# Weights of an attention and gated feed-forward kernel stored raw in the first batch and split in the second, with four small edits around the scores and the softmax

## The chip, the cores and the metric

The kernel runs on one NeuronCore of one Trainium2 chip. The metric is the device time of one launch in microseconds (us), taken as the median of three runs. TensorE is called PE here, its weight loads PEld, VectorE DVE, ScalarE ACT, GpSimd POOL; SP is the queue from which nearly all DMAs are issued.

## The reference

Causal attention over 4 batches, 12 heads, 448 positions and a head size of 64, then a gated feed-forward block of width 1536 on the 1792 rows of 768:

```python
scores = scale * np.matmul(q, k.transpose(0, 1, 3, 2))
scores = np.where(mask, -1000000000.0, scores)
scores = scores - np.max(scores, axis=-1, keepdims=True)
attn = np.exp(scores)
attn = attn / (np.sum(attn, axis=-1, keepdims=True) + 1e-09)
x = np.matmul(attn, v)   # regrouped to (4*448, 768)
g = x @ w_gate
out = (g * (1.0 / (1.0 + np.exp(-g))) * (x @ w_val)) @ w_out
```

All inputs and the output are float32.

## The kernel before, in words

**Precision.** Most products are made with two float32r parts: a number is copied to float32r (its high part), the copy is subtracted from the number (its low part), and a product takes three matmuls: high by high, high by low, low by high. In the code this is `mm3` (L871) for the feed-forward block and the list `passes` (L486) for the scores. Batch 0's attention alone works in plain float32 (`NS`, `NP`, L30).

**Stages.** The four batches are worked one after another. A batch has twelve attention units, one for each head, that come in pairs; the feed-forward block of a batch takes its 768 rows of attention output `xs`, split into `xh` and `xl` (L785), and runs 24 column groups `M` (L888) and six output groups `MO` (L924). Attention of batch c+1 is interleaved with the feed-forward block of batch c.

**One attention unit.** PE makes the scores S (L485). DVE adds the mask and takes the row maximum (L548), ACT takes the exponential and sums each row into a tile `sums` (L563), DVE adds 1e-9 and takes the reciprocal `rec` (`recip`, L573 to L577), ACT or POOL or DVE multiplies by it (L607 to L617), PE transposes the result into a PSUM tile T (L694), and the transposed probabilities are split into `ph` and `pl` (`spread`, L627). The next transposes use the same PSUM bank, so they wait until DVE has read T for `pl`. Then PE multiplies with the values (L734). `sums` and `rec` are rings of `NR` rows; unit u uses row u mod NR.

**Weights.** A feed-forward group needs one 128 by 768 block of weights in two parts, `whl` (five buffers). The weights arrive 64 bits wide in `wide` (three buffers); ACT or POOL takes the upper part (`upper`, L851), DVE joins it with the lower (`lower`, L854) into the float32 block `wraw` (two buffers), and `split` (L811) copies and subtracts. This is done for the 36 blocks in batch 0. `RAW` (L46) is the list of batches that split their weights and store both parts to a scratch in HBM (`keep`, L820): with `[0]`, batch 0 stores 768 KB for each block, and the batches 1 to 3 load 768 KB for each block and split nothing. A batch ahead of the one in `RAW` stores the float32 block alone (`wr`, 384 KB).

**What sets the order.** A planner (`Planner.run`, L104) places every operation on an engine by due times and a table of costs (`cost`, L64; `TURN`, L42, for changes between kinds of work on PE), picks the engine where several are allowed, and writes one order for all engines. Each engine and the SP queue run theirs strictly in that order; waits are on semaphores. So a change in the costs moves instructions everywhere.

**The start.** 22 small bfloat16 matmuls on a tile of ones (`WARM`, L279) run on PE while the first inputs load. Then come the scores of the first unit pair, then those of the second.

**Short blocks.** The queries are cut at 64, 192, 320 and 448. The first block has 64 rows only; its weight load is made `FEW` = 72 columns wide (L504), as is that of the low parts of the probabilities against the values (L740).

Of the kernel before, what the change touches and what calls it, by code (L numbers as in the profile page):

```python
# [8 lines left out]
F32 = mybir.dt.float32  # L9
# [8 lines left out]
P = 128  # L18
# [2 lines left out]
CUTS = [[0, 64, 192, 320, 448], [0, 64, 192, 320, 448], [0, 64, 192, 320, 448], [0, 64, 192, 320, 448]]  # L21
WID = [0, 64, 192, 320, 448]
CHUNKS = [[(0, 0, 448)], [(1, 0, 448)], [(2, 0, 448)], [(3, 0, 448)]]
NR = 8
SLOPE0 = 1.0
WLEAD = 1.2
XD = [-10.0, 3.0]
# [11 lines left out]
SHARED = 0.5  # L39
PVLATE = 0  # L40
LAT = {"PE": 0.29, "DVE": 0.2, "ACT": 0.23, "POOL": 0.2, "SP": 0.1}
TURN = {'ms': 0.19, 'sm': 0.19, 'mt': 0.0, 'tm': 0.0, 'ts': 0.19, 'st': 0.19, 'mv': 0.15, 'vm': 0.15, 'tv': 0.15, 'vt': 0.15, 'sv': 0.15, 'vs': 0.15, 'om': 0.055, 'os': 0.1, 'so': 0.19, 'ot': 0.03}  # L42
TS = 0.0
PF = 1.12
GF = 1.25
RAW = [0]  # L46
SG = [[[0, 3]], [[1, 2]]]
TV = 0.0
WINDOW = 96
SPARE = [2]  # L50
FEW = 72
WARM = 22
FIRST = [[[0, 1]], [[2]], [[3]]]
KBUS = 1 / 320
DLAT = 1.8
# [8 lines left out]
def cost(e, kind, n):  # L64
    if e == "ACT":
        return {"psum": 66, "sbuf": 110, "ptr": 190, "exp": 280, "tanh": 160}[kind] / 1e3 + n / 1200
    if e == "DVE":
        return 0.075 + n / {"one": 1920}.get(kind, 960)
    if e == "POOL":
        return {"one": 190, "ptr": 260, "two": 180}[kind] / 1e3 + n / {"two": 465.0}.get(kind, 1200.0)  # L70
    return {"r": max(n * 0.4475e-3 + 0.0025, 0.109), "n": n / 600, "t": n * 0.109 / 128}[kind] + 0.001


class Res:
# [154 lines left out]
def kernel(  # L229
# [33 lines left out]
    masks = cpool.tile([P, P + maskX + P], F32, tag="masks", name="masks")  # L263
    back, mask = masks[:, : maskX + P], masks[:, P:]
    both = cpool.tile([P, D], F32, tag="both", name="both")
    all_sums = cpool.tile([P, NR, NKC], F32, tag="sums", name="sums")
    sums = [all_sums[:, i] for i in range(NR)]
    all_rec = cpool.tile([P, NR, NKC], F32, tag="rec", name="rec")
    rec = [all_rec[:, i] for i in range(NR)]
    xs = [cpool.tile([P, T], F32, tag=f"xs{i}", name=f"xs{i}") for i in range(KD)]  # L270
    xh = [cpool.tile([P, T], F32R, tag=f"xh{i}", name=f"xh{i}") for i in range(KD)]
# [4 lines left out]
    ones = xs[0][:, : P // 2]  # L276
    nc.vector.memset(ones, 1.0)
    warm = bank("O", "warm")
    for _ in range(WARM):  # L279
        nc.tensor.matmul(warm[:, :P], ones.bitcast(BF16), ones.bitcast(BF16), start=True, stop=True)  # L280
    cpool.tile([P, 32], F32, tag="pad", name="pad")
    top = cpool.tile([P, WC], U32, tag="top", name="top")
    nc.vector.memset(top, 0)
    nc.vector.memset(all_sums, 1.0)
    make_identity(nc, ident)
    nc.gpsimd.memset(masks, 0.0)
    for m_, step, base in ((back, 1, 1 - P), (mask, -1, maskX)):
# [104 lines left out]
    def attention(u):  # L392
# [76 lines left out]
        if h % 2 == 0:  # L469
# [10 lines left out]
            for gi_, sess in enumerate(FIRST if rest else SG if c == 0 else [sum(SG, [])]):  # L480
# [4 lines left out]
                def score(gi_=gi_, sess=sess, steps=steps, tags=tags):  # L485
                    passes = ((None, None),) if U.ns else ((0, 0), (0, 1), (1, 0))  # L486
                    for x, blks in enumerate(sess):
                        for y in (0, 1):
                            B_, off = bank(tags[x], f"S{u + y}_{gi_}_{x}"), 0
                            for i in blks:  # L490
                                q1_ = U.qi[i][1][1]
                                st[u + y][f"S{i}"] = B_[:, off : off + q1_]
                                off += q1_
                    for i in steps:
                        q0, q1_ = U.qi[i][1]
                        for z, (a, b_) in enumerate(passes):
                            for y in (0, 1):
                                half = slice(D * y, D * y + D)
                                Q = s["qw"][half] if U.ns else s["Q"][half, a]
                                K = s["kw"][half] if U.ns else s["K"][half, b_]  # L500
                                if U.joint and i == 0:
                                    nc.tensor.matmul(st[u]["S0"][half], Q[:, :D], K[:, :D] if y else K[:, S - D :], start=True, stop=True)
                                    continue
                                r = max(U.rows[i], FEW)  # L504
                                nc.tensor.matmul(st[u + y][f"S{i}"][:r], Q[:, q0 : q0 + r],  # L505
                                                 K[:, :q1_] if y else K[:, S - q1_ :], start=z == 0, stop=z == len(passes) - 1)
                ws = [U.qi[i][1][1] for i in steps]
                if U.ns:
                    so = op({"PE": (sum(cost("PE", "n", w) + 0.06 for w in ws) + TS, score), "kind": "s"}, due(2),
                            (rest if gi_ else some) or [lq, lk], list(rSs.values()), [rq, rk])  # L510
                else:
                    so = op({"PE": (sum(3 * cost("PE", "r", w) for w in ws) + TS, score), "kind": "s"}, due(2), sp,
                            list(rSs.values()), [rQ, rK])
                for x, blks in enumerate(sess):
                    for i in blks:
# [56 lines left out]

        def recip():  # L573
            i0, i1 = U.own[0][0], U.own[-1][0] + 1
            sm, rc = sums[u % NR][:, i0:i1], rec[u % NR][:, i0:i1]
            nc.vector.tensor_scalar(rc, sm, 1.0e-9, None, ALU.add)
            nc.vector.reciprocal(rc, rc)  # L577
        rc = op({"DVE": (0.3, recip)}, due(5), exps, [], [rsum])

# [138 lines left out]
    def weigh(u):  # L718
# [6 lines left out]
        if not npv:  # L725
            rO, dps, use, dur = Res("O"), [], [], 0.0
            for g, o_, w, _, stk, d_, r_ in (blocks[j] for j in range(nj)):
                dps += [x for x in d_ if x not in dps]
                use += [r for r in r_ if r not in use]
                dur += (1 if stk else 2) * cost("PE", "r", w)  # L730

            todo = [(j, "ph") for j in (0, *range(2, nj))] + [(j, "pl") for j in range(nj - 1, 0, -1)] + [(1, "ph")]

# [282 lines left out]
```

## Time and profile before

| | |
|---|---|
| median of three runs | 683.66 us (683.42 to 683.88) |
| the profiled execution, its own time | 684.65 us |
| its span, first to last instruction | 682.9 us |
| PE matmul busy | 671.8 us, 98% of the span |
| PE weight loads busy | 598.9 us, 88% |
| DVE, ACT, POOL busy | 356.7 us, 347.8 us, 193.7 us |
| moved by DMA | 165.08 MB, 242 GB/s over the span |

The profile is one execution. Busy matmul time is modelled, since matmuls overlap. The idle time in front of an instruction is shown with what released it. The mean over the span hides the stages: batch 0's weights are prepared in the first third, and the last fifth has feed-forward work alone.

### The profile page before, as it was taken

How to read it: one execution, taken by the hardware profiler on the slowest of the kernel's cores; microseconds unless marked ns; L12 is line 12 of the kernel's file. 1: busy time of each engine (PE TensorE's matmuls, PEld its weight loads, DVE VectorE, ACT ScalarE, POOL GpSimd, SP SyncE). 2: the span in 40 equal slices, each digit the busy share in tenths (PEclk: the TensorE clock that was granted, in tenths of full speed). 3: DMA queues.
4: the chain of work that ended last, by engine and by line, in shares of the span. 5: the costliest groups of instructions: out<-in, count | busy, mean ns of one | idle time of the engine just before them, and what ended most of it. 6: DMA issues, size and time to landing. Idle time of an engine off the chain costs nothing.

```text
span 682.9 us, 10861 instructions
## 1 busy us (share of the span) xinstructions
PE 671.8 (98%) x3898; PEld 598.9 (88%) x3898; DVE 356.7 (52%) x881; ACT 347.8 (51%) x864; POOL 193.7 (28%) x238
## 2 busy tenths in 40 slices
PE   9999999999999999999999999999999999999998
PEld 6567898899888999999999989999999999999997
DVE  5777889898788464355633346545444222222100
ACT  6998688687798363245634336346345211111000
POOL 3766455556162130031322214134232000000000
PEclk9999999999999999999999999999999999999999
DMA  8878899999988865556667665554555675676771
GB/s 293 277 260 308 303 352 390 321 374 314 347 309 324 320 202 201 191 176 215 202 223 239 201 230 189 200 186 139 186 198 164 216 224 213 223 229 212 226 251 41
DMA packets 40118, 165.08 MB, mean 242 GB/s; under 512 B 4480, under 2 KB 13952, under 8 KB 40064
## 3 DMA queue, kind: packets, MB, share of 16 engines
q1 hardware_dynamic: 39904, 164.28, 70.6%
q8 instruction: 31, 0.51, 0.3%
q14 instruction: 23, 0.19, 0.1%
q10 hardware_dynamic: 160, 0.10, 0.1%
HBM read 130.55 MB, written 33.82 MB: 241 GB/s over the span
## 4 chain that ended last, share of the span: by engine, by line
PE 81%; ACT 11%; DVE 6%; issue 1%; POOL 0%; ACTq 0%; DVEq 0%
PE M L874 15%; PE M L875 15%; PE M L876 15%; PE MO L874 8%; PE MO L875 8%; PE MO L876 7%; PE S L505 4%; PE O L741 4%; ACT p L565 4%; PE T L699 3%; ACT p L609 2%; ACT ph L311 1%; ACT top L311 1%; DVE wraw L857 1%; PE T L667 1%
## 5 line engine op out<-in xcount | busy, mean ns | idle before, releaser
L874 PE MATMUL M<-xh,whl 128*128 128x448 f32 x576 | 215.0, 373 | 0.0
L875 PE MATMUL M<-xl,whl 128*128 128x448 f32 x576 | 209.4, 364 | 0.0
L876 PE MATMUL M<-xh,whl 128*128 128x448 f32 x576 | 209.1, 363 | 0.0
L874 PEld LDWEIGHTS M<-xh,whl 128*128 128x128 f32 x576 | 108.2, 188 | 8.5 <-issue 1.7
L876 PEld LDWEIGHTS M<-xh,whl 128*128 128x128 f32 x576 | 108.1, 188 | 7.7
L875 PEld LDWEIGHTS M<-xl,whl 128*128 128x128 f32 x576 | 108.4, 188 | 6.8 <-DVE xl L333 0.3
L874 PE MATMUL MO<-hh,whl 128*128 128x448 f32 x288 | 107.2, 372 | 0.0
L876 PE MATMUL MO<-hh,whl 128*128 128x448 f32 x288 | 104.6, 363 | 0.6 <-DVE whl L333 0.6
L875 PE MATMUL MO<-hl,whl 128*128 128x448 f32 x288 | 104.7, 364 | 0.0
L565 ACT ACTIVATE p<-p,m 128x192 f32<-128x192 f32 (+3 forms) x180 | 91.1, 509 | 3.4 <-DVE m L553 3.3
L311 ACT ACTIVATE ph<-T 128x384 fp32r<-128x384 f32 (+3 forms) x116 | 57.8, 504 | 56.5 <-PE T L667 34.4
L553 DVE CUSTOM_DVE_ANT_0 p<-S,masks 128x192 f32<-128x192 f32 (+3 forms) x180 | 68.3, 426 | 21.4 <-PE S L505 20.2
L311 ACT ACTIVATE hh<-t 128x448 fp32r<-128x448 f32 x40 | 23.1, 577 | 82.0 <-DVE t L917 82.0
L609 ACT ACTIVATE p<-p,rec 128x192 f32<-128x192 f32 (+3 forms) x130 | 58.8, 502 | 9.3 <-DVE rec L577 9.0
L911 DVE SCALAR_TENSOR_TENSOR t<-t,M 128x448 f32<-128x448 f32 x48 | 29.7, 619 | 57.2 <-ACT t L907 56.8
L876 PEld LDWEIGHTS MO<-hh,whl 128*128 128x128 f32 x288 | 54.0, 188 | 4.7 <-DVE whl L333 1.0
L874 PEld LDWEIGHTS MO<-hh,whl 128*128 128x128 f32 x288 | 54.1, 188 | 4.5 <-issue 1.2
L875 PEld LDWEIGHTS MO<-hl,whl 128*128 128x128 f32 x288 | 54.2, 188 | 3.6 <-DVE hl L333 0.3
L917 DVE TENSOR_TENSOR t<-t,M 128x448 f32<-128x448 f32 x48 | 29.6, 618 | 51.0 <-PE M L876 50.6
L907 ACT ACTIVATE t<-M 128x448 f32<-128x448 f32 x48 | 26.0, 542 | 57.5 <-PE M L876 56.9
L333 DVE TENSOR_TENSOR pl<-T,ph 128x384 fp32r<-128x384 f32 x72 | 39.6, 550 | 22.6 <-ACT ph L311 22.3
L699 PE MATMUL T<-ident,p 128*128 128x128 f32 x288 | 46.8, 276 | 3.3 <-DVE pl L333 3.0
(80 smaller groups left out, 822.7 us busy)
## 6 DMA issues: line engine op xcount, KB each, us to landing
whl<-ws SPq DMA_DIRECT2D x108, 768.0 KB, 4.4
wide<-in_w_dram SPq DMA_DIRECT2D x36, 768.0 KB, 6.8
ws<-whl SPq DMA_DIRECT2D x36, 768.0 KB, 7.5
vraw<-in_v_dram SPq DMA_DIRECT2D x24, 256.0 KB, 4.3
out_dram<-osb SPq DMA_DIRECT2D x24, 224.0 KB, 4.7
qraw<-in_q_dram SPq DMA_DIRECT2D x23, 224.0 KB, 4.6
kraw<-in_k_dram SPq DMA_DIRECT2D x23, 224.0 KB, 4.6
qraw<-in_q_dram SPq DMA_DIRECT2D x1, 128.0 KB, 2.5
```

The source lines that it names most:

```text
L311: nc.scalar.activation(out(), in_(), AF.Copy, scale=scale)
L333: r["DVE"] = (cost("DVE", "two", n), lambda: nc.vector.tensor_tensor(out(), a(), b(), alu))
L505: nc.tensor.matmul(st[u + y][f"S{i}"][:r], Q[:, q0 : q0 + r], K[:, :q1_] if y else K[:, S - q1_ :], start=z == 0, stop=z == len(passes) - 1)
L553: nc.vector.tensor_tensor_reduce(p[:r], s[f"S{i}"][:r], mask[:r, maskX - q0 : maskX - q0 + q1_] if h % 2 else back[:r, P - min(q1_, P) : P ...
L565: nc.scalar.activation(p[:r], p[:r], AF.Exp, bias=peak(i)[:r], scale=-1.0, accum_out=sums[u % NR][:r, i : i + 1],)
L609: nc.scalar.activation(p[:r], p[:r], AF.Copy, scale=rec[u % NR][:r, i : i + 1])
L699: nc.tensor.transpose(pt[:, o_ + q0 - bs : o_ + q0 - bs + r], s[f"p{i}"][:r, k0 : k0 + P], ident[:r, :r])
L874: nc.tensor.matmul(out[:, :n], a[:, w], xhi, start=first, stop=False)
L875: nc.tensor.matmul(out[:, :n], a[:, w], xlo, start=False, stop=False)
L876: nc.tensor.matmul(out[:, :n], l[:, w], xhi, start=False, stop=last)
L911: nc.vector.scalar_tensor_tensor(t, t, 1.0, ps[c, f, 0][:, :N], ALU.add, ALU.mult)
L917: nc.vector.tensor_tensor(t, t, ps[c, f, 1][:, :N], ALU.mult)
```

## The change

In batch 0 each weight block is now stored as one float32 block of 384 KB. Batch 1 loads that block, splits it again (36 copies and 36 subtractions of 128 by 768) and stores both parts; the batches 2 and 3 load both parts as before. Eight more small matmuls follow the first unit pair's scores. The addition of 1e-9 becomes a sum of pairs: a row `NR` of `sums` holds 1e-9, and a `tensor_reduce` adds that row to the unit's row; NR goes from 8 to 7. `FEW` goes from 72 to 66. The planner has other costs for changes between kinds of work on PE, for the 64-wide scores and for the products with the values.

```diff
-NR = 8
+NR = 7
-TURN = {'ms': 0.19, 'sm': 0.19, 'mt': 0.0, 'tm': 0.0, 'ts': 0.19, 'st': 0.19, ...
+TURN = {'ms': 0.15, 'sm': 0.17, 'mt': 0.0, 'tm': 0.0, 'ts': 0.15, 'st': 0.17, ...
-RAW = [0]
+RAW = [1]
-FEW = 72
+FEW = 66
+WARM2 = 8
...
-    return {"r": max(n * 0.4475e-3 + 0.0025, 0.109), "n": n / 600, "t": n * 0.109 / 128}[kind] + 0.001
+    return {"r": max(n * 0.4475e-3 + 0.0025, 0.109), "f": n * 0.4475e-3 + 0.0045, "n": n / 600, "t": n * 0.109 / 128}[kind] + 0.001
...
-    all_sums = cpool.tile([P, NR, NKC], F32, tag="sums", name="sums")
+    all_sums = cpool.tile([P, NR + 1, NKC], F32, tag="sums", name="sums")
...
+    busy(WARM)
...
-    nc.vector.memset(all_sums, 1.0)
+    nc.vector.memset(all_sums[:, :NR], 1.0)
+    nc.vector.memset(all_sums[:, NR], 1.0e-9)
...
+                    if u == 0 and i in FIRST[-1][0]:
+
+                        busy(WARM2)
...
-                    so = op({"PE": (sum(3 * cost("PE", "r", w) for w in ws) + TS, score), "kind": "s"}, due(2), sp,
+                    so = op({"PE": (sum(3 * (0.062 if w == D else cost("PE", "r", w)) for w in ws) + TS, score), "kind": "s"}, due(2), sp,
...
-            sm, rc = sums[u % NR][:, i0:i1], rec[u % NR][:, i0:i1]
-            nc.vector.tensor_scalar(rc, sm, 1.0e-9, None, ALU.add)
+
+            sm, rc = all_sums[:, u % NR :: NR - u % NR, i0:i1], rec[u % NR][:, i0:i1]
+            nc.vector.tensor_reduce(rc, sm.rearrange("p a c -> p c a"), mybir.AxisListType.X, ALU.add)
             nc.vector.reciprocal(rc, rc)
...
-                dur += (1 if stk else 2) * cost("PE", "r", w)
+                dur += (1 if stk else 2) * cost("PE", "f", w)
```

The order moves on every engine. Three places follow.

DVE at the end of batch 0's weights (before): `whl33` to `whl35` are the low parts of the last three blocks, `p24` the masked scores of the first unit of batch 2, `ph22_0` and `ph23_0` the low parts of the transposed probabilities of the last unit pair of batch 1.

```order
408 L553 ISA m25_2715 128x1
409 L333 TENSOR_TENSOR whl33_2694<-wraw33_2683,whl33_2694 128x768
410 L553 ISA p24_3_2675,m25_2715<-S25_0_0_2607,masks_67 128x448
411 L553 ISA m25_2715 128x1
412 L857 SCALAR_TENSOR_TENSOR wraw34_2756<-wide34_2592,top_138 128x768
413 L576 TENSOR_SCALAR rec_70<-sums_69 128x4
414 L577 RECIPROCAL rec_70<-rec_70 128x4
415 L333 TENSOR_TENSOR whl34_2765<-wraw34_2756,whl34_2765 128x768
416 L857 SCALAR_TENSOR_TENSOR wraw35_2817<-wide35_2640,top_138 128x768
417 L545 MEMSET p26_0_2824 64x128
418 L333 TENSOR_TENSOR ph22_0_2815<-T23_0_2780,ph22_0_2815 64x448
419 L333 TENSOR_TENSOR ph23_0_2820<-T23_0_2780,ph23_0_2820 64x448
```

The same place after the change:

```order
400 L339 TENSOR_TENSOR pl22_1_2653<-T22_1_2625,ph22_1_2644 128x384
401 L867 SCALAR_TENSOR_TENSOR wraw34_2661<-wide34_2475,top_138 128x768
402 L339 TENSOR_TENSOR whl33_2642<-wraw33_2620,whl33_2642 128x768
403 L339 TENSOR_TENSOR pl22_2_2691<-T22_2_2664,ph22_2_2684 128x384
404 L867 SCALAR_TENSOR_TENSOR wraw35_2700<-wide35_2580,top_138 128x768
405 L339 TENSOR_TENSOR whl34_2686<-wraw34_2661,whl34_2686 128x768
406 L339 TENSOR_TENSOR xl4_87<-xs4_75,xh4_81 128x448
407 L339 TENSOR_TENSOR whl35_2709<-wraw35_2700,whl35_2709 128x768
408 L554 MEMSET p26_0_2741 64x128
409 L339 TENSOR_TENSOR ph22_0_2743<-T23_0_2728,ph22_0_2743 64x448
410 L339 TENSOR_TENSOR ph23_0_2749<-T23_0_2728,ph23_0_2749 64x448
411 L339 TENSOR_TENSOR whl36_2755<-wraw36_2719,whl36_2755 128x768
```

The last blocks of batch 0 now come ahead of the scores of unit 24, and all of them, up to `whl35`, ahead of `ph22_0`; before, unit 24 and 25 stood in front of `whl33`.

DVE in batch 1 (before), where unit 27's T bank is read: `t1_4` is the gated product of feed-forward group 4, `xs1` the attention output.

```order
499 L333 TENSOR_TENSOR ph27_0_3379<-T27_0_3364,ph27_0_3379 64x448
500 L333 TENSOR_TENSOR hl4_105<-t1_4_3350,hh4_93 128x448
501 L333 TENSOR_TENSOR xs1_72<-O26_3392,tmp26_3407 64x448
502 L333 TENSOR_TENSOR pl27_1_3421<-T27_1_3403,ph27_1_3414 128x384
503 L333 TENSOR_TENSOR pl27_2_3445<-T27_2_3426,ph27_2_3435 128x384
```

The same place after the change:

```order
497 L339 TENSOR_TENSOR ph27_0_3365<-T27_0_3347,ph27_0_3365 64x448
498 L339 TENSOR_TENSOR whl48_3372<-wraw48_3307,whl48_3372 128x768
499 L320 TENSOR_SCALAR ph27_1_3398<-T27_1_3389 128x384
500 L339 TENSOR_TENSOR xs1_72<-O26_3378,tmp26_3393 64x448
501 L339 TENSOR_TENSOR pl27_1_3413<-T27_1_3389,ph27_1_3398 128x384
502 L339 TENSOR_TENSOR whl49_3419<-wraw49_3360,whl49_3419 128x768
503 L339 TENSOR_TENSOR pl27_2_3442<-T27_2_3421,ph27_2_3431 128x384
```

A subtraction of 128 by 768 now stands in front of `ph27_1` and another between `pl27_1` and `pl27_2`. In the whole of batch 1, DVE has 33 such subtractions and POOL 3; ACT has 23 of the copies and POOL 13.

PE near the end of batch 0's attention (before): T9 are the transposes of unit 9, O9 its product with the values, M0_1 a feed-forward group of batch 0.

```order
196 L699 MATMUL T9_2_782<-ident_66,p8_2_615 128x128
197 L699 MATMUL T9_2_782<-ident_66,p8_3_618 128x128 x2
198 L874 MATMUL M0_1_792<-xh0_77,whl1_607 128x448
199 L875 MATMUL M0_1_792<-xl0_83,whl1_607 128x448
200 L876 MATMUL M0_1_792<-xh0_77,whl1_607 128x448
201 L772 MATMUL O9_800<-ph9_0_786,vraw8_547 64x64 x2
```

The same place after the change:

```order
212 L709 MATMUL T9_2_783<-ident_66,p8_2_621 128x128
213 L709 MATMUL T9_2_783<-ident_66,p8_3_605 128x128 x2
214 L782 MATMUL O9_798<-ph9_0_788,vraw8_555 64x64 x2
215 L782 MATMUL O9_798<-ph9_0_788,vraw8_555 64x384 x2
```

The three feed-forward matmuls between the transposes and the product are gone from there; they come later.

## Rows read from the trace of the kernel before

**Rows 1.** The page, busy time and share of the span by engine.

```profile
PE 671.8 (98%) x3898; PEld 598.9 (88%) x3898; DVE 356.7 (52%) x881; ACT 347.8 (51%) x864; POOL 193.7 (28%) x238
```

**Rows 2.** Stretches: busy us of PE, PEld, DVE, ACT, POOL; clock, DMA share, GB/s.

```profile
193.00:226.00 33.00, 31.51 (x210) 27.61 (x210) 28.29 (x73) 30.38 (x83) 15.74 (x18) 1.00 0.89 316
226.00:280.00 54.00, 54.00 (x297) 50.03 (x296) 25.66 (x60) 20.33 (x47) 8.31 (x14) 1.00 0.65 221
```

**Rows 3.** Waits of PE: engine, line, releaser, us in total, times, longest.

```profile
PE T L699 <- DVE pl L333: 3.0, 4, 1.4
```

**Rows 4.** Lines 576 and 577: duration in ns, shortest, median, longest.

```profile
L576 DVE TENSOR_SCALAR rec<-sums x48: 151/170/1625, 9.3 to 527.8; 128x4 f32<-128x4 f32 x42, 128x3 f32<-128x3 f32 x6
...
L577 DVE RECIPROCAL rec<-rec x48: 175/178/179, 9.5 to 528.0; 128x4 f32<-128x4 f32 x42, 128x3 f32<-128x3 f32 x6
```

**Rows 5.** Timeline near 67 us: start, length, engine, line, then idle time before.

```profile
66.55 1.82 POOL L336 TENSOR_TENSOR whl<-wraw,whl 128x768 fp32r<-128x768 f32 x1
...
66.78 1.62 DVE L576 TENSOR_SCALAR rec<-sums 128x4 f32<-128x4 f32 x1 [0.18 <-ACT p L565]
...
69.20 0.30 PE L699 MATMUL T<-ident,p 128*128 128x128 f32 x1 [1.40 <-DVE pl L333]
```

**Rows 6.** Timeline near 396 us.

```profile
395.12 1.14 DVE L576 TENSOR_SCALAR rec<-sums 128x4 f32<-128x4 f32 x1
...
397.06 0.30 PE L699 MATMUL T<-ident,p 128*128 128x128 f32 x1 [0.64 <-DVE pl L333]
```

**Rows 7.** Timeline near 502 us.

```profile
501.24 0.77 DVE L576 TENSOR_SCALAR rec<-sums 128x4 f32<-128x4 f32 x1
...
502.81 0.41 PE L699 MATMUL T<-ident,p 128*128 128x128 f32 x2 [0.28 <-DVE pl L333]
```

**Rows 8.** Timeline near 210 to 218 us.

```profile
209.81 1.01 DVE L576 TENSOR_SCALAR rec<-sums 128x4 f32<-128x4 f32 x1 [0.19 <-ACT p L565]
...
215.17 1.72 DVE L333 TENSOR_TENSOR whl<-wraw,whl 128x768 fp32r<-128x768 f32 x1
...
218.36 0.55 PE L699 MATMUL T<-ident,p 128*128 128x128 f32 x3 [0.65 <-DVE pl L333]
```

**Rows 9.** Timeline near 203 us.

```profile
202.11 1.91 DVE L333 TENSOR_TENSOR whl<-wraw,whl 128x768 fp32r<-128x768 f32 x1
...
204.06 0.47 PE L876 MATMUL MO<-hh,whl 128*128 128x448 f32 x1 [0.62 <-DVE whl L333]
```

**Rows 10.** Timeline of PE at the start, and the same scores near 27 us.

```profile
0.98 2.53 PE L280 MATMUL warm<-xs 128*128 128x128 bf16 x22 [0.98 <-DVE xs L277]
...
8.54 0.48 PE L502 MATMUL S<-kraw,qraw 64*64 64x64 f32 x4 [0.61 <-DVE m L553]
8.95 3.57 PE L505 MATMUL S<-kraw,qraw 64*128 64x448 f32 x12
...
27.35 1.89 PE L505 MATMUL S<-kraw,qraw 64*128 64x448 f32 x12
```

**Rows 11.** Weight loads by shape: busy us, mean ns of one.

```profile
L505 PEld LDWEIGHTS S<-KS,QS 64*128 64x128 f32 x324 | 22.7, 186 | 0.3
...
L505 PEld LDWEIGHTS S<-KS,QS 64*72 64x72 f32 x108 | 4.8, 139 | 4.6 <-issue 4.6
```

**Rows 12.** The subtractions of the weights on DVE, all in batch 0.

```profile
L333 DVE TENSOR_TENSOR whl<-wraw,whl 128x768 fp32r<-128x768 f32 x28 | 31.6, 1129 | 0.9 <-ACT whl L311 0.9
...
L333 DVE TENSOR_TENSOR whl<-wraw,whl x28: 928/951/1916, 35.2 to 215.2; 128x768 fp32r<-128x768 f32 x28
```

**Rows 13.** DMA issues: count, KB each, median us to landing.

```profile
ws<-whl SPq DMA_DIRECT2D x36, 768.0 KB, 7.5
```

**Rows 14.** Timeline of PE near 45 us: two feed-forward matmuls, then O9.

```profile
45.05 0.37 PE L875 MATMUL M<-xl,whl 128*128 128x448 f32 x1
45.26 0.37 PE L876 MATMUL M<-xh,whl 128*128 128x448 f32 x1
45.91 1.78 PE L772 MATMUL O<-ph,vraw 64*64 64x64 f32 x12 [0.28 <-ACT ph L311]
```

More of the change, by code (lines that the diff above doesn't have):

```diff
@@ L41 @@
 LAT = {"PE": 0.29, "DVE": 0.2, "ACT": 0.23, "POOL": 0.2, "SP": 0.1}
-TURN = {'ms': 0.19, 'sm': 0.19, 'mt': 0.0, 'tm': 0.0, 'ts': 0.19, 'st': 0.19, 'mv': 0.15, 'vm': 0.15, 'tv': 0.15, 'vt': 0.15, 'sv': 0.15, 'vs': 0.15, 'om': 0.055, 'os': 0.1, 'so': 0.19, 'ot': 0.03}
+TURN = {'ms': 0.15, 'sm': 0.17, 'mt': 0.0, 'tm': 0.0, 'ts': 0.15, 'st': 0.17, 'mv': 0.15, 'vm': 0.15, 'tv': 0.15, 'vt': 0.15, 'sv': 0.15, 'vs': 0.15, 'om': 0.0, 'os': 0.1, 'so': 0.16, 'ot': 0.0}
 TS = 0.0
@@ L265 @@
     both = cpool.tile([P, D], F32, tag="both", name="both")
-    all_sums = cpool.tile([P, NR, NKC], F32, tag="sums", name="sums")
+    all_sums = cpool.tile([P, NR + 1, NKC], F32, tag="sums", name="sums")
     sums = [all_sums[:, i] for i in range(NR)]
-    all_rec = cpool.tile([P, NR, NKC], F32, tag="rec", name="rec")
+    all_rec = cpool.tile([P, NR + 1, NKC], F32, tag="rec", name="rec")
     rec = [all_rec[:, i] for i in range(NR)]
@@ L278, with busy @@
     warm = bank("O", "warm")
-    for _ in range(WARM):
-        nc.tensor.matmul(warm[:, :P], ones.bitcast(BF16), ones.bitcast(BF16), start=True, stop=True)
+    def busy(n):
+        for _ in range(n):
+            nc.tensor.matmul(warm[:, :P], ones.bitcast(BF16), ones.bitcast(BF16), start=True, stop=True)
+    busy(WARM)
     cpool.tile([P, 32], F32, tag="pad", name="pad")
```

## The prediction

> **What bounds the kernel now.** I read the page first: PE is busy for 671.8 of the span's 682.9 us [rows 1], so what can be won is mostly PE's remaining waits, at whatever engine they end. The list of PE's waits shows where: the largest group is the transposes that wait for DVE to finish `pl`, 3.0 us in four waits, the longest 1.4 us [rows 3]. A transpose needs the PSUM bank that DVE reads for `pl`. The busy times by stretch then show how much room the other engines have. At the end of batch 0's weights, from 193 to 226 us, DVE is busy for 28.29 of 33 us and PE is not full (31.51); in the first third of batch 1, from 226 to 280 us, DVE is busy for 25.66 of 54 us and PE is full [rows 2]. So in batch 0 DVE is nearly a second bound, and in batch 1 it has half its time left.
>
> Last I looked at what DVE did in front of the four waits for `pl`. The addition of 1e-9 works on four numbers in each partition and has a median of 170 ns, but up to 1625 [rows 4]. In the timeline the long ones stand beside a POOL instruction and end with it: one that starts at 66.78 lasts to 68.40, and the POOL subtraction beside it, 66.55 plus 1.82, ends at 68.37 [rows 5]. The reciprocal right after it, on the same four numbers, has 175 to 179 ns in all 48 cases [rows 4]. So the addition is held by POOL and the reciprocal is not.
>
> **The change, part by part.** The profiled execution took 684.65 us, its span 682.9; the median of the runs is 683.66, 0.99 lower. I work out a difference from the rows and take it off either.
>
> *The sum of pairs.* It replaces an addition that POOL can hold. No row shows a `tensor_reduce`. The nearest is the reciprocal: the same engine, the same size, one input in SBUF, never held [rows 4]. I price the reduction at 0.18 us. Its worst end is that it is held like the addition, which leaves everything as it is. Three waits of PE follow a held addition directly, since `pl` stands right behind it on DVE: 1.40 us at 69.20, where the addition took 1.62 and so 1.45 us more than its median [rows 5]; 0.64 us at 397.06, with 1.14 and so 0.97 too much [rows 6]; 0.28 us at 502.81, with 0.77 and so 0.60 too much [rows 7]. In each the excess is larger than the wait, so the wait goes: 2.32 us. The fourth, 0.65 us at 218.36, has a held addition of 1.01 us eight us earlier, but also a weight subtraction of 1.72 us just before [rows 8]; an excess of 0.84 would cover it, if the delay is carried that far. I count it: together -3.0 us. The bounds are 0 and -4.0, the latter if delays that ended in no visible wait of PE in batch 0 go too. Next late behind them is then ACT's copy `ph`, which `pl` needs.
>
> The Trainium skill, "SBUF — State Buffer", section "Who interferes with whom", states that a `tensor_reduce` on this chip never contends with GpSimd, while a `tensor_scalar` between SBUF operands can take the port pair that the two share. No run here shows the first yet; by that rule the bound of 0 falls away and the term is the -3.0 or more. "VectorE: DVE Perf Modes", section "Rules for kernel authors", speaks against the edit: it calls `tensor_reduce` the slowest DVE operation and advises to restructure it away from a hot path. By that one the reduction would be longer than the addition: at twice its median, an estimate, 0.17 us more at each of the four places, and the term -2.3 instead of -3.0.
>
> *The weights of batch 0.* The store shrinks from 768 KB with 7.5 us to landing [rows 13] to half of that, and it no longer holds one of the five `whl` buffers, only one of two `wraw`. So the last blocks can be split sooner: in the order, `whl33` to `whl35` now stand ahead of unit 24's scores. PE's wait of 0.62 us at 204.06 for a weight subtraction that took 1.91 us [rows 9] should go: -0.6, bounds 0 and -0.7. A `wraw` buffer that stays held until its store lands could make DVE wait; the 36 blocks are split between 35 and 215 us [rows 12], 5 us each, so the buffer is wanted again some 10 us later, and even the larger store lands in 7.5; I cost it at nothing. Without that cover each late store would cost DVE what it is late.
>
> *The weights of batch 1.* 36 copies and 36 subtractions are added, 33 of the latter on DVE. Batch 0 had 28 there, at a mean of 1129 ns, a median of 951 and up to 1916 [rows 12]: they too are held at times. 33 of 1.13 are 37 us on an engine that is half free, so the cost lies in the moments, not in the total. `pl` and `ph` queue behind them on DVE, and PE's next transposes wait for `pl`. The 28 in batch 0 left two waits on PE, 0.62 [rows 9] and 0.65 [rows 8], 1.27 us; 33 at that rate give 1.5. Since DVE is much emptier in batch 1, I take +1.0. The lower bound is 0. The upper is the whole excess of mean over median passed on to PE: 33 times 0.178, 5.9 us. The loads halve in batch 1 and a store of 768 KB is added; the DMA share there is 0.65 against 0.89 in the stretch before [rows 2], so this is hidden by spare bandwidth; without it, copies would wait at the head of ACT's and POOL's queues and put off `ph`.
>
> *The small matmuls.* The twelve larger score matmuls of the second unit pair take 3.57 us from 8.95 on; the same twelve take 1.89 us at 27 us [rows 10]. The first thus run at about half the clock (1.2 GHz against 2.4). PE was busy before them, but idle for 0.61 us just ahead [rows 10]. Eight matmuls at the pace of the 22 (2.53 us, 0.115 each) fill 0.9 us there. If they keep PE busy enough for the full clock to come before these scores, 1.7 us go (3.57 less 1.89); if the clock comes when it did, 0.9 in a gap of 0.61 costs 0.3. I take half of the gain, since the rise may come midway and the softmax of the first units then bounds: -0.9, bounds +0.3 and -1.7.
>
> *The narrower loads.* A load of 72 columns takes 139 ns, one of 128 takes 186 [rows 11]: 0.84 ns for a column, 5 ns for six. There are 108 of them in the scores and 108 in the products. If only those of the scores count, half of them since two heads run side by side: 54 times 5, 0.27 us. I take -0.3, bounds 0 and -0.8 (54 and 108 of them).
>
> *The order.* In batch 0, O9 now follows its transposes with no feed-forward matmuls between. Before, three of those stood there and PE still waited 0.28 us for ACT's `ph` [rows 14]; without them the wait grows by their length, three times the 0.21 from one's start to the next's [rows 14]: +0.6, bounds 0 and +1.2 (a second such place). Other places move too; I have no row for them.
>
> The sum: -3.0 - 0.6 + 1.0 - 0.9 - 0.3 + 0.6 = -3.2 us. From 684.65 that is 681.45 for a profiled execution, and **680.5 us** as a median of runs.
>
> **The rivals.** A measurement of this kernel can tell 0.2%, 1.37 us, from no change: faster is below 682.29, slower above 685.03.
>
> *Batch 1's subtractions cost more than all the rest brings.* They stand between `ph` and `pl` in the order shown. Each may be held by POOL, as those of batch 0 were [rows 12], and then PE's transposes come late. Without batch 1 the sum is -4.2. Each case that PE feels costs 0.62 [rows 9]. From nine of the 33 on, the change is slower by over 0.2% (9 times 0.62 is 5.6); with eleven it gives 686.3. For it speaks that every unit has such places; against it that the same work at a DVE load of 86% left only two waits, while batch 1 has 48% [rows 2] and some 70% with the addition. The same section of the Trainium skill states that a DVE instruction with two SBUF inputs contends with a GpSimd instruction that reads SBUF. The trace agrees: the subtraction of 1.91 us [rows 9].
>
> *The held time moves on.* The addition is no longer held, but POOL's work now collides with the subtractions in front of `pl`, or ACT's `ph` is late, so that the sum of pairs brings 0.8 and not 3.0: 682.7, within 0.2% or next to it.
>
> *All goes well.* The clock rises early (-1.7), the sum of pairs gives -4.0, batch 0 -0.7, the loads -0.5, and batch 1 costs nothing: -6.9, or 676.8.
>
> *The small matmuls don't do what they are for*, and the clock rises when it did: +0.3 for -0.9, 681.7. This lies within the forecast.
>
> **How the numbers follow.** The forecast, with its terms within their bounds, 678.5 to 682.3: 0.50. All goes well, below 678.5: 0.18. The held time moves on, or terms cancel, 682.3 to 685.0: 0.20. Batch 1 costs too much: 0.12. So faster 0.68, same 0.20, slower 0.12. The range reaches from the well-going case, 676.5, to 684.8, which takes in the moved time and leaves out the slow case and a little at the lower end.
>
> **What would show it.** In the profile after, the line of the sum of pairs should have a mean near 0.18 us and no long ones; PE's waits for `pl` after a long `rec` should be gone; the second pair's scores should take clearly less than 3.57 us; PE should not wait for `whl` near 204 us; and PE's waits between 226 and 385 us should sum to about 1 us. I am wrong if the reductions are held like the additions, if PE waits for `pl` or `ph` behind a `whl` subtraction in batch 1 time after time, or if the start is no shorter and the middle makes up for nothing.

## The result, and the profile after

The change makes the kernel slower: a median of 688.61 us (687.65 to 689.68, five runs) against 683.88 us (683.42 to 685.04, five runs) of the kernel before on the same chip, a ratio of 1.007 with a 95% interval of 1.0054 to 1.0086. That is +4.7 us where -3.2 was forecast. The profiled execution took 688.6 us, its span 686.8, 3.9 more than the span before.

Three points of the timeline say in which stage the time went: the first feed-forward matmul of batch 0, the first of batch 3 (from here on PE has feed-forward work alone), and the end of PE's last matmul.

| us | batch 0 starts | batch 3 starts | PE ends | last stage |
|---|---|---|---|---|
| before | 41.81 | 549.69 | 679.45 | 129.76 |
| after | 39.39 | 549.04 | 683.11 | 134.07 |

The start is 2.4 us shorter, the middle 1.8 longer, and the last stage 4.3 longer. In the last stage the two kernels do the same: 648 matmuls, no attention, no weights to split. A step, below, is the time from the start of one matmul to the start of the next. The timeline of PE at 600 us, of the kernel before (columns: start, length, engine, line, operation, tiles, shape):

```profile
599.69 0.36 PE L875 MATMUL M<-xl,whl 128*128 128x448 f32 x1
599.89 0.36 PE L876 MATMUL M<-xh,whl 128*128 128x448 f32 x1
600.09 0.36 PE L874 MATMUL M<-xh,whl 128*128 128x448 f32 x1
600.29 0.36 PE L875 MATMUL M<-xl,whl 128*128 128x448 f32 x1
```

The same view of the changed kernel:

```profile
599.67 0.37 PE L886 MATMUL M<-xh,whl 128*128 128x448 f32 x1
599.88 0.37 PE L884 MATMUL M<-xh,whl 128*128 128x448 f32 x1
600.08 0.37 PE L885 MATMUL M<-xl,whl 128*128 128x448 f32 x1
600.29 0.37 PE L886 MATMUL M<-xh,whl 128*128 128x448 f32 x1
```

Read the starts: 0.60 us for three steps before, 0.62 after. At full resolution every step of the last stage is 200 ns before, and 207, 207, 206 in turn after, 206.67 on average. No wait shows, and both runs have a granted clock of 0.999. I call this the pace. In both traces it is set within the first few matmuls of a stretch of feed-forward matmuls and is then kept: of the 116 stretches before and 120 after, one alone changes its pace later, where PE waits for `whl` at 204 us of the kernel before. The beginning of the last stretch in the changed kernel:

```profile
546.64 0.52 PE L751 MATMUL O<-pl,VS 128*66 128x128 f32 x3
547.00 0.34 PE L751 MATMUL O<-ph,VS 128*128 128x384 f32 x1
547.18 0.37 PE L884 MATMUL MO<-hh,whl 128*128 128x448 f32 x1
547.38 0.37 PE L885 MATMUL MO<-hl,whl 128*128 128x448 f32 x1
547.59 0.37 PE L886 MATMUL MO<-hh,whl 128*128 128x448 f32 x1
```

The last unit's products, with the 66-column loads, stand directly ahead. Counting the steps of 206 or 207 ns between neighbouring feed-forward matmuls over the whole trace gives 199 before and 1081 after, 655 of them in this last stretch. 882 steps more at 6.67 ns are 5.9 us: more than the whole loss. The 227 of them that lie ahead of the last stretch make 1.5 us, by the same count, and the middle has lost 1.8.

The signs that the prediction named are nearly all there. The sum of pairs (L586) of the changed kernel, minimum, median and maximum in ns, where the addition of [rows 4] had 151, 170 and 1625:

```profile
L586 DVE TENSOR_REDUCE rec<-sums x48: 145/156/165, 9.3 to 527.4; 128x4 f32<-128x8 f32 x42, 128x3 f32<-128x6 f32 x6
```

The start of PE, against [rows 10]: the second pair's twelve scores take 2.00 us instead of 3.57.

```profile
7.77 1.04 PE L283 MATMUL warm<-xs 128*128 128x128 bf16 x8
8.74 0.48 PE L508 MATMUL S<-kraw,qraw 64*64 64x64 f32 x4
9.15 2.00 PE L511 MATMUL S<-kraw,qraw 64*128 64x448 f32 x12
```

PE's waits after (waiter, releaser: us in total, times, longest), against [rows 3]:

```profile
PE O L751 <- DVE ph L339: 2.8, 3, 1.5
...
PE O L751 <- DVE pl L339: 0.6, 1, 0.6
PE T L709 <- DVE pl L339: 0.5, 1, 0.5
```

The waits of transposes for `pl` have shrunk from 3.0 to 0.5 us, and none is for `whl`. But products now wait 2.8 us for `ph`, in batch 0, where the kernel before had 1.2; and all waits of PE in that view, but for the one of the first small matmuls, come to 6.6 us after and 6.3 before. So the changed kernel has about as many waits as before, in other places. Between 226 and 385 us the one wait is that of 0.53 us for `pl`, at 337.43. And the chain that ended last has a member that it lacked before, the landing of `wr<-wraw` with 2%; `wraw` on DVE has 2% where it had 1%:

```profile
PE M L884 14%; PE M L885 14%; PE M L886 14%; PE MO L884 8%; PE MO L885 8%; PE MO L886 8%; PE S L511 6%; PE O L751 4%; PE T L709 4%; DMA wr<-wraw 2%; ACT p L574 2%; DVE wraw L867 2%; PE O L782 1%; PE T L677 1%; ACT p L619 1%
```

### The profile page after: what moved, and what is told of

It reads as the page before. It is cut to its first block, busy times and chain, and to the rows that moved or that the text cites. A ratio compares the mean times of both kernels' runs of the same rounds, so it can differ in the third digit from the quotient of the medians.

```text
span 686.8 us, 10966 instructions
## 1 busy us (share of the span) xinstructions
PE 675.3 (98%) x3906; PEld 597.8 (87%) x3906; DVE 379.4 (55%) x925; ACT 360.1 (52%) x875; POOL 219.1 (32%) x256
## 4 chain that ended last, share of the span: by engine, by line
PE 85%; ACT 5%; DVE 5%; DMA 2%; issue 2%; POOL 1%; SPq 0%; DVEq 0%; ACTq 0%; POOLq 0%
PE M L884 14%; PE M L885 14%; PE M L886 14%; PE MO L884 8%; PE MO L885 8%; PE MO L886 8%; PE S L511 6%; PE O L751 4%; PE T L709 4%; DMA wr<-wraw 2%; ACT p L574 2%; DVE wraw L867 2%; PE O L782 1%; PE T L677 1%; ACT p L619 1%
## 5 line engine op out<-in xcount | busy, mean ns | idle before, releaser
L317 ACT ACTIVATE ph<-T 128x384 fp32r<-128x384 f32 (+3 forms) x95 | 47.5, 510 | 52.4 <-PE T L677 27.3
L339 DVE TENSOR_TENSOR whl<-wraw,whl 128x768 fp32r<-128x768 f32 x58 | 56.0, 966 | 9.9 <-ACT whl L317 8.2
L619 ACT ACTIVATE p<-p,rec 128x448 f32<-128x448 f32 (+3 forms) x130 | 58.7, 513 | 5.2 <-DVE rec L587 5.2
```

The costliest lines, as they stand in the source:

```text
L317: nc.scalar.activation(out(), in_(), AF.Copy, scale=scale)
L339: r["DVE"] = (cost("DVE", "two", n), lambda: nc.vector.tensor_tensor(out(), a(), b(), alu))
L619: nc.scalar.activation(p[:r], p[:r], AF.Copy, scale=rec[u % NR][:r, i : i + 1])
```

## Experiments on the pace

The first theory: the 66-column loads of the products set the longer pace. Its rival: the slowdown comes from batch 1's subtractions or from the new order.

**The changed kernel with 72 columns.**

```diff
-FEW = 66
+FEW = 72
```

> The changed kernel with loads of 72 columns again, all else as changed. Pace theory: the step from one feed-forward matmul to the next is 200 ns or 206.7 ns, it is set where a stretch of them begins and then kept, and the 66-column loads of the products set the longer one. The changed kernel has 1081 steps at 206 or 207 ns, the kernel before 199; 882 times 6.67 ns is 5.9 us. So about 682.7 us here, 0.2% below the kernel before, and nearly all 660 matmuls of the last stretch at 200 ns. Rival (the loss is in batch 1's subtractions or in the order): at most 0.5 us from the changed kernel's 688.6.

Measured: 682.79 us, ratio to the kernel before 0.9974 (0.996 to 0.9988). 167 long steps are left, none in the last stretch. The rival falls as the cause of the slowdown: 5.8 us of the changed kernel's time was this one number, and without it the change is a small gain.

**The kernel before with 66 columns.**

```diff
-FEW = 72
+FEW = 66
```

> The kernel before with loads of 66 columns, all else as before. Pace theory: at least the last stretch of 660 matmuls goes to 206.7 ns, 4.4 us, and up to 5.9 in all: 688.3 to 689.8 us. By the prediction's term for the narrower loads: 683.4 to 683.6. Rival (the loss lies elsewhere in the change): 683.4 to 684.

Measured: 688.64 us, ratio 1.0068 (1.0053 to 1.0083). 1137 long steps, 658 of them in the last stretch. The number alone costs 4.65 us, though each load is shorter, as was forecast: 137 ns here, against 144 before, for one in the products. The 938 long steps more make 6.3 us; 5.2 of them show in the span of the profiled execution, 4.3 in its last stage, and where the rest comes back was not traced.

**72 columns in the products alone.**

```diff
-                    m = FEW if t == "pl" else 2 * D
+                    m = 72 if t == "pl" else 2 * D
```

> The changed kernel with loads of 72 columns in the products alone, 66 in the scores. If the products' loads just ahead of the feed-forward matmuls set the pace: as the first run, 682.4 to 682.9. If the scores' loads do it: as the changed kernel, 688.6.

Measured: 682.21 us, ratio 0.9973 (0.9953 to 0.9992), 182 long steps. It is the loads of the products; those of the scores do no harm.

**72 columns in three of the changed kernel's 3906 matmuls**, the ones ahead of the last stretch.

```diff
-                    m = FEW if t == "pl" else 2 * D
+                    m = (72 if u == len(units) - 1 else FEW) if t == "pl" else 2 * D
```

> The changed kernel with loads of 72 columns in three matmuls only, those of the last unit's products, which stand ahead of the last stretch of 657 feed-forward matmuls. Pace theory: 655 steps go from 206.7 to 200 ns, 4.4 us: 684.2 us. If the pace is not set there: 688.6.

Measured: 684.22 us, ratio 1.0 (0.9986 to 1.0015). The last stretch of this kernel begins so:

```profile
545.36 0.53 PE L751 MATMUL O<-pl,VS 128*72 128x128 f32 x3
545.72 0.33 PE L751 MATMUL O<-ph,VS 128*128 128x384 f32 x1
545.89 0.36 PE L884 MATMUL MO<-hh,whl 128*128 128x448 f32 x1
546.09 0.36 PE L885 MATMUL MO<-hl,whl 128*128 128x448 f32 x1
```

Steps of 200 ns, and no long one up to the end; 419 are left in the stages ahead. Six columns more in three loads took off 4.4 us.

**Other widths.** Each second group of products, those that feed-forward matmuls follow, loads another width; the base is the kernel before with the sum of pairs.

```diff
+WIDTHS = {1 + 2 * k: x for k, x in enumerate([64, 68, 70, 74, 76, 80, 88, 96] * 2)}
+WIDTHS[35] = 128
...
-                    m = FEW if t == "pl" else 2 * D
+                    m = few if t == "pl" else 2 * D
```

> The kernel before with the sum of pairs, where every second group of products (those that feed-forward matmuls follow) loads another number of columns: 64, 68, 70, 74, 76, 80, 88, 96 in turn, twice, and 128 in the last. Each stretch of feed-forward matmuls shows its pace by itself. If loads that are short in time set the longer step: 64, 68 and 70 give 206.7 ns, 74 and more 200 ns. If what counts is that the number of columns divides by 8: 68, 70, 74 and 76 give 206.7, 64, 80, 88, 96 and 128 give 200. If only the very number 72 is good: all give 206.7. The pace of each width should be the same in both of its places.

There is one execution of this kernel (685.92 us), and it serves for its trace alone. Matmuls in the stretch behind each group, and how many of its steps are long:

| columns | first place | second place |
|---|---|---|
| 64 | 18, none | 6, none |
| 68 | 9, none | 6, none |
| 70 | 30, 28 long | 9, none |
| 74 | 33, none | 42, none |
| 76 | 27, none | 24, none |
| 80 | 15, none | 27, none |
| 88 | 21, 19 long | 24, 23 long |
| 96 | 21, none | 24, none |
| 128 | 660, 658 long | |

All three rules that I had offered fall. Short loads (64, 68) are harmless, 88 and 128 do harm though they divide by 8, and 70 comes out differently in its two places. The group with 128 columns and what follows:

```profile
543.51 0.62 PE L747 MATMUL O<-pl,VS 128*128 128x128 f32 x3
...
544.14 0.37 PE L880 MATMUL MO<-hh,whl 128*128 128x448 f32 x1
544.35 0.37 PE L881 MATMUL MO<-hl,whl 128*128 128x448 f32 x1
```

So a width is not good or bad by itself. That the stretch takes its pace from how PE's loads and matmuls stand to each other when it begins is my guess, and not shown. Products are not alone in setting it: in the kernel before, from 220 us on, all twelve stretches that follow four transposes in a row go over to the long pace after their first three matmuls, and of those that follow three transposes all but one take the short one; in the changed kernel the first holds for seven of twelve. What in PE makes the two paces stays open.

## Experiments on the other parts

**The sum of pairs alone**, on the kernel before.

```diff
-NR = 8
+NR = 7
...
-            nc.vector.tensor_scalar(rc, sm, 1.0e-9, None, ALU.add)
+            nc.vector.tensor_reduce(rc, sm.rearrange("p a c -> p c a"), mybir.AxisListType.X, ALU.add)
```

> The kernel before with the sum of pairs alone (tensor_reduce of a sum and 1e-9), the order of all other instructions unchanged. The prediction's term: -3.0 us, bounds 0 and -4.0: about 681.0 us. Theory that the changed kernel's trace gives: its 48 reductions take 145 to 165 ns and none is held, so the waits of 1.40, 0.64 and 0.28 us behind a held addition go; but the held time may move on to the next instruction of DVE, since the POOL subtraction beside it is still there, and then less than 1.5 us are won: 682.5 to 683.7.

Measured: 678.33 us, ratio 0.9926 (0.9913 to 0.9938): -5.5 us, beyond the bound of -4.0. DVE and POOL at the place of [rows 5]:

```profile
64.33 0.16 DVE L577 TENSOR_REDUCE rec<-sums 128x4 f32<-128x8 f32 x1
...
64.62 0.53 DVE L334 TENSOR_TENSOR pl<-T,ph 128x384 fp32r<-128x384 f32 x1
65.07 1.70 DVE L334 TENSOR_TENSOR whl<-wraw,whl 128x768 fp32r<-128x768 f32 x1
...
64.10 1.85 POOL L337 TENSOR_TENSOR whl<-wraw,whl 128x768 fp32r<-128x768 f32 x1
```

The reduction and `pl` pass beside POOL's 1.85 us. The held time has moved on, to the subtraction of `whl` that takes 1.70 us where [rows 12] have a median of 0.951; but it stands behind `pl`, so PE doesn't wait. The longest waits of PE that are left behind the start:

```profile
PE O L742 <- DVE ph L334: 0.8, 1, 0.8
...
PE T L700 <- DVE pl L334: 0.4, 1, 0.4
PE MO L877 <- DVE whl L334: 0.3, 1, 0.3
```

From the first feed-forward matmul of batch 0 to that of batch 3 this kernel takes 502.9 us (39.9 to 542.8), the kernel before 507.9. Some 3.6 of these 5.0 us are in the two lists of waits; the rest was not traced.

**The small matmuls alone**, on the kernel before.

```diff
+WARM2 = 8
...
+                    if u == 0 and i in FIRST[-1][0]:
+                        busy(WARM2)
```

> The kernel before with the eight small matmuls behind the first scores alone. The prediction's term: -0.9 us, bounds +0.3 and -1.7. Theory from the changed kernel's start: the second pair's twelve larger scores take 2.0 instead of 3.57 us, so the start is shorter by 1.4 us or a little more: 682.2 to 682.7. Rival: the softmax of the first units bounds the start, and less than 0.5 us comes through: 683.5 to 684.

Measured: 683.96 us, ratio 1.0002 (0.9994 to 1.0011): nothing. Yet the second scores took 1.90 us in its profile. The clue is in executions without the small matmuls. In the run above, with the sum of pairs alone, and in the next one:

```profile
8.45 1.89 PE L506 MATMUL S<-kraw,qraw 64*128 64x448 f32 x12
```

```profile
4.33 1.90 PE L505 MATMUL S<-kraw,qraw 64*128 64x192 f32 x12
8.66 0.33 PE L502 MATMUL S<-kraw,qraw 64*64 64x64 f32 x4 [2.43 <-DVE rec L576]
8.93 1.89 PE L505 MATMUL S<-kraw,qraw 64*128 64x448 f32 x12
```

In the second of these even the first pair's scores ran at the faster level, and PE then stood for 2.43 us for the softmax. The traces' records of the granted clock begin with its full level (2.4 GHz) at 12.6 us before, at 9.25 in this run, at 7.3 and 4.4 in the two executions shown. In the one trace of each kernel, the full level begins between 4.4 and 13.4 us in the eight without these matmuls, and between 4.7 and 9.4 in the six with them. So the clock rises at different times though PE's instructions at the start are alike: the 3.57 us in the profile of before was one execution, not the rule. The small matmuls may cut off the latest rises; in the median of the runs that is worth nothing.

**The weights moved to batch 1 alone**, on the kernel before.

```diff
-RAW = [0]
+RAW = [1]
```

> The kernel before with weights stored as float32 in batch 0 and split and stored in batch 1, all else as before (the planner sets a new order). The prediction's terms: -0.6 for batch 0 and +1.0 for batch 1, together +0.4: 684.4. Theory from the changed kernel's trace: in batch 0 the wraw buffer is held until its store lands, DVE stands for the landing five times (5.5 us in all) where it is nearly a second bound, and PE waits more there, while batch 1 adds only the 0.5 us of one wait: 684.5 to 686. Rival (fewer bytes stored let batch 0 go faster): 682 to 683.5.

Measured: 687.06 us, ratio 1.0043 (1.003 to 1.0056): +3.25 us, more than the theory of held buffers had at its upper end. The profiled execution is the fastest of the five (684.97 us), so that its trace shows little of the loss. Three of PE's waits in it, of 0.76 us at 130.20, 1.09 at 158.21 and 0.98 at 201.34, come back in the next run.

**The same on top of the sum of pairs.**

```diff
-RAW = [0]
+RAW = [1]
...
-            nc.vector.tensor_scalar(rc, sm, 1.0e-9, None, ALU.add)
+            nc.vector.tensor_reduce(rc, sm.rearrange("p a c -> p c a"), mybir.AxisListType.X, ALU.add)
```

> The kernel before with the sum of pairs and the weights moved to batch 1, the planner's costs as before. If the two parts add up: 678.3 plus 3.25, 681.6. If the moved weights cost mainly by the additions that POOL's longer work holds: about 679.

Measured: 683.61 us, ratio 0.9998 (0.9983 to 1.0013): 5.3 us above the sum of pairs alone. The two don't add up; the moved weights take the whole gain back. Of the 5.3 us this trace shows 3.9 as waits: from the first feed-forward matmul of batch 0 on PE waits for 5.4 us here (gaps over 0.1 us), against 1.5 with the sum of pairs alone, and all but 0.14 of it before 202 us. DVE at 97 to 102 us, and the products behind it:

```profile
98.17 0.61 DVE L912 SCALAR_TENSOR_TENSOR t<-t,M 128x448 f32<-128x448 f32 x1
100.70 0.96 DVE L858 SCALAR_TENSOR_TENSOR wraw<-wide,top 128x768 uint32<-128x768 uint32 x1 [1.92 <-DMA wr<-wraw]
```

```profile
102.36 0.65 PE L742 MATMUL O<-ph,VS 128*128 128x448 f32 x3 [1.67 <-DVE ph L334]
```

DVE stands for 1.92 us at the instruction that joins the next block into `wraw`, until a store of `wraw` (`wr<-wraw`) has landed: that of an earlier block, which still reads the buffer. `ph` is queued behind it, and PE waits 1.67 us for `ph`. The other three large waits of this kernel, of 0.74 us at 130.13, 1.14 at 158.14 and 1.12 at 201.32, stand behind instructions of DVE with two inputs that POOL holds: two joins into `wraw`, of 2.18 and 2.47 us where the median before was 0.96, and a subtraction. Here is that of 158 us:

```profile
155.17 2.27 DVE L334 TENSOR_TENSOR hl<-t,hh 128x448 fp32r<-128x448 f32 x1
157.47 1.28 DVE L334 TENSOR_TENSOR ph<-T,ph 64x448 fp32r<-64x448 f32 x2
...
154.67 2.29 POOL L337 TENSOR_TENSOR whl<-wraw,whl 128x768 fp32r<-128x768 f32 x1
```

A subtraction that takes 0.61 us elsewhere takes 2.27 beside POOL's 2.29, this time ahead of `ph`. The Trainium skill, "SBUF — State Buffer", section "Who interferes with whom", has both halves: an instruction of DVE with two SBUF inputs contends with a GpSimd instruction that reads SBUF, a `tensor_reduce` on this chip never does. This trace agrees with the first (2.27 us), that of the changed kernel with the second (48 reductions, 165 ns at most).

**The planner's new costs alone**, on the kernel before.

```diff
-                dur += (1 if stk else 2) * cost("PE", "r", w)
+                dur += (1 if stk else 2) * cost("PE", "f", w)
...
-                    so = op({"PE": (sum(3 * cost("PE", "r", w) for w in ws) + TS, score), "kind": "s"}, due(2), sp,
+                    so = op({"PE": (sum(3 * (0.062 if w == D else cost("PE", "r", w)) for w in ws) + TS, score), "kind": "s"}, due(2), sp,
```

(and the new `TURN`, and the definition of the cost `f`.)

> The kernel before with the planner's new costs alone (times of turning from one kind of PE work to another, of the products and of the narrow scores), which only set another order. The prediction's term for the order: +0.6 us, bounds 0 and +1.2: 684.4. Theory from the eighth run (with the sum of pairs and the small matmuls too, 683.9 where these two alone would give 678.4): the new order itself costs 4 to 6 us: 688 to 690. Rival: the order costs little by itself and takes away the gain of the sum of pairs: 683.5 to 684.5.

Measured: 688.96 us, ratio 1.0072 (1.006 to 1.0084): +5.3 us from nothing but another order. Batch 3 starts at 554.0 us, 4.3 later than before, though batch 0 starts 2.9 earlier. Its longest waits:

```profile
PE MO L876 <- DVE whl L333: 2.0, 2, 1.7
PE T L699 <- DVE pl L333: 1.9, 4, 0.7
```

Behind the longest of them the granted clock falls to half (1.2 GHz) for 3.4 us, which no other trace of this case shows between its start and its end; in the 4.4 us ahead PE was busy for 2.61. PE at that place, and the two stretches in the columns of [rows 2]:

```profile
207.16 0.47 PE L876 MATMUL MO<-hh,whl 128*128 128x448 f32 x1 [1.68 <-DVE whl L333]
...
210.18 0.57 PE L874 MATMUL MO<-hh,whl 128*128 128x448 f32 x1
210.55 0.57 PE L875 MATMUL MO<-hl,whl 128*128 128x448 f32 x1
```

```profile
204.00:208.40 4.40, 2.61 (x15) 1.65 (x13) 3.84 (x9) 4.36 (x13) 3.65 (x4) 1.00 0.97 332
208.40:211.80 3.40, 3.40 (x12) 3.19 (x13) 2.29 (x4) 2.44 (x7) 1.29 (x2) 0.50 0.74 265
```

3.4 us at half the clock are some 1.7 us of the 5.3, an estimate from these rows, so that wait seems to cost more than its length; in four of the five runs the mean granted clock is 0.997.

**The changed kernel with 72 columns and both parts stored in batch 0.**

```diff
-RAW = [1]
+RAW = [0]
...
-FEW = 66
+FEW = 72
```

> The changed kernel with loads of 72 columns and with both weight parts stored in batch 0 as before (the planner sets a new order). With 72 columns alone it was 682.8. If the weights' move costs net +0.4 as predicted: 682.4. If the held wraw buffers cost 1 to 2 us in batch 0: 681 to 682. If the move gains: above 683.

Measured: 683.91 us, ratio 1.0006 (0.9995 to 1.0016). With the weights moved this kernel was 682.79, so in the new order the move gains about 1.1 us by the medians (about 2 by the two ratios), where it costs 3.25 in the old one. And the new order again costs some 5.5 us, against the sum of pairs alone.

**The version that the experiments point to**: the kernel before, the sum of pairs, 66 columns in the scores alone.

```diff
-                                r = max(U.rows[i], FEW)
+                                r = max(U.rows[i], 66)
...
```

(and the sum of pairs, as above.)

> The kernel before with the sum of pairs, and loads of 66 columns in the scores alone, 72 in the products. Pace theory: as the sum of pairs alone, 678.3, less the 0.3 us of the prediction for the scores' loads: 678.0, and no stretch that follows products at 206.7 ns. If the scores' loads also set the longer step: up to 683.

Measured: 677.59 us, ratio 0.9908 (0.9895 to 0.9921): 6.1 us below the kernel before and 11 below the changed one. No stretch behind products is long. Its interval overlaps that of the sum of pairs alone, so what the scores' loads bring by themselves is not resolved.

## Why the prediction was wrong

The forecast was faster, and no rival gave the true cause. The terms of its sum, against the runs of one part each on the kernel before:

| term | forecast | bounds | measured alone |
|---|---|---|---|
| sum of pairs | -3.0 | 0, -4.0 | -5.5 |
| weights, both batches | +0.4 | -0.7, +5.9 | +3.25 |
| small matmuls | -0.9 | +0.3, -1.7 | +0.15, no change |
| narrower loads | -0.3 | 0, -0.8 | +4.65 |
| the order | +0.6 | 0, +1.2 | +5.3 |
| sum | -3.2 | | +7.85; all together +4.7 |

**The narrower loads** is the step that failed, and alone it turns the sign: with 72 columns the changed kernel is at 0.9974. The prediction priced what a load of 66 columns saves, 0.3 us, and set 0 as the worst end. No row spoke for that end: that the loads could change the step of the matmuls behind them was not thought of, and was put at nothing without a reason. The loads did get shorter. What they do to the matmuls behind them costs 4.65 us alone and 5.8 in the changed kernel, fifteen to twenty times the 0.3.

**The sum of pairs** was right in its mechanism and too small. The reductions are never held, and the waits of [rows 5 to 7] are gone. The wait of [rows 8], counted as gone, is 0.4 us in that run, and that of [rows 9], counted with the weights, 0.3; but from batch 0 to batch 3 the time fell by 1.4 us more than the waits in the lists, so that the bound of -4.0 was too near. What that rest is stays open; the start of its profile is 1.9 us shorter too, with the early rise of the clock. The warning of the Trainium skill that I had set beside it, "VectorE: DVE Perf Modes", section "Rules for kernel authors", that a reduction is the slowest operation of DVE, shows no price at this size: a median of 156 ns against the addition's 170.

**The weights.** "I cost it at nothing", for the `wraw` buffer held by its store, was wrong: the argument that a buffer is wanted some 10 us later, and a store lands in 7.5, left no room for blocks that are split in quick succession. DVE waits for a landing of `wr` five times in the changed kernel, 5.5 us in all. Two of these reach PE, with 0.60 us and 0.73. One of them, and PE's wait behind it:

```profile
137.12 0.96 DVE L867 SCALAR_TENSOR_TENSOR wraw<-wide,top 128x768 uint32<-128x768 uint32 x1 [2.01 <-DMA wr<-wraw]
...
139.47 0.57 PE L751 MATMUL O<-pl,VS 128*66 128x128 f32 x3 [0.60 <-DVE pl L339]
```

The longest wait of the changed kernel, 1.49 us at 104.04, stands behind a join into `wraw` that isn't late but held, beside a subtraction on POOL (its median before was 0.96):

```profile
99.65 1.46 POOL L342 TENSOR_TENSOR hl<-t,hh 128x448 fp32r<-128x448 f32 x1 [3.16 <-ACT hh L317]
...
100.02 1.92 DVE L867 SCALAR_TENSOR_TENSOR wraw<-wide,top 128x768 uint32<-128x768 uint32 x1
...
104.04 0.62 PE L751 MATMUL O<-ph,VS 128*128 128x448 f32 x3 [1.49 <-DVE ph L339]
```

Batch 1, for which I had taken +1.0, has a single wait of 0.53 us. DVE's load there is what was forecast, some 70% (38.27 of 54 us), as the busy times of the second stretch of [rows 2] show for the changed kernel (PE, PEld, DVE, ACT, POOL, clock, DMA share, GB/s):

```profile
226.00:280.00 54.00, 54.00 (x322) 49.25 (x321) 38.27 (x90) 34.09 (x86) 18.97 (x27) 1.00 0.86 295
```

And the subtractions of the changed kernel are hardly held: 58 of them on DVE take 966 ns on average, where the 28 of [rows 12] took 1129. So the rival of eleven slow subtractions fell. The waits of the moved weights are in batch 0, here and in the run with the sum of pairs, the stage that the prediction itself called nearly bound by DVE.

**The order** was priced by one place that I had rows for. That place is near the forecast: the products wait 0.68 us for `ph`, against the 0.28 of [rows 14], 0.4 more where 0.6 was forecast. But the sentence "Other places move too; I have no row for them" was left without a bound, and those places are worth some +5 us in the old surroundings, the fall of the clock among them. That a new order draws anew which instructions meet POOL's long ones ahead of `ph`, `pl` or `whl` fits its waits; they were not traced one by one.

**The small matmuls** fell to a reading of one profile: the late rise of the clock in it was taken as the rule. Their own bounds, +0.3 and -1.7, hold the measured +0.15.

The terms don't add up to the measured time: 7.85 against 4.7. The sum of pairs, the small matmuls and the order do add up: -0.05, against +0.1 for the kernel that has the three. Two crossings are measured: in the new order the moved weights gain 1.1 us instead of costing 3.25, and the 66 columns cost 5.8 us instead of 4.65. Why the moved weights and the new order suit each other was not taken apart; the traces show only that the waits for `whl` at 195 and 204 us, 1.6 us in the run with both parts stored in batch 0, are gone with the weights moved.

## What to carry to other kernels

Where PE runs one kind of matmul for hundreds of instructions, read the step between starts, not the busy share: three per cent of a stage hid in it here with no wait in any view, and three matmuls ahead of the stretch set it. When a change touches several things and a planner lays out the order anew, make one kernel of each part before judging the whole: here a gain of 5.5 us was buried under three losses, one of them an edit of one number. And an instruction of DVE that POOL can hold is worth replacing with one that it can't, above all where a second instruction that PE waits for is queued behind it.

## What the hardware showed that I had not expected

The same stream of weight loads and matmuls of 448 columns runs at either 200 or 206.67 ns a step, at the same granted clock, and keeps its pace over as many as 660 matmuls; six columns in three loads, in the last 0.6 us ahead of it, were enough to change which. The Trainium skill, "TensorE: Matmul & The Clock Gate", section "Back-to-back issue gap", gives N / 2.4 + 2.5 ns at the full clock as the gap of an isolated matmul, an estimate of 189 ns for 448 columns, and says that it over-counts for a stream at large N. The traces differ: they show two paces, both longer.

Some kernels with the weights moved also spread more from one execution to the next: 679.98 to 684.29 us for the changed kernel with 72 columns (eleven runs) and 681.35 to 687.18 for the sum of pairs with the weights moved (twelve), against 683.39 to 684.45 for the small matmuls alone (eleven). The slowest of the twelve has a mean granted clock of 0.998, so a fall of the clock may be part of it; the cause was not sought.
